# Linear attention and a mixture of experts: chunks attended in pairs, tokens transposed in idle banks

## Chip, cores, metric

One NeuronCore of a Trainium2 chip runs the whole kernel as one program. The metric is the device time of an execution in microseconds (us), least is best; the median of the runs shown is used.

## What is computed

Attention with decay over 4 batches of 768 tokens, 8 heads of 64, and on its output x (3072 tokens of 512) a mixture of 8 experts, of which each token uses the best:

```
for b in range(nb):
    intra = einsum('bhic,bhjc->bhij', qb, kb) * Dmask     # Dmask[i,j] = lam**(i-j) for i >= j
    intra = einsum('bhij,bhjd->bhid', intra, vb)
    inter = einsum('bhid,bhde->bhie', qb * lam_pow, kv_state)
    out[:, :, sl] = intra + inter
    kv_state = lam_block * kv_state + einsum('bhsd,bhse->bhde', kb * rev_pow, vb)
...
logits = x @ w_gate + modality_bias[modality_id]
e_idx = argmax(logits, axis=1)
for e in range(E):
    mask = e_idx == e
    h = maximum(x[mask] @ w1[e], 0.0)
    out[mask] = gate_w[mask, None] * (h @ w2[e])
...
```

gate_w is the softmax weight of the chosen expert; w1 is 512 x 1024 and w2 1024 x 512 for each expert.

## The kernel before

The engines: TensorE (PE; PEld loads its weights), VectorE (DVE), ScalarE (ACT), GpSimd (POOL), SyncE (SP, issues most DMAs). PSUM has eight banks of 128 x 512 float32 in which PE writes.

The attention takes 24 chunks of 128 tokens (six a batch), one in each step of a loop over g. A step has, on PE: the scores of chunk g (L224, 64 x 128 tiles, into two banks named s); what chunk g − 1 reads from the carried state (L267, bank o; not for the first chunk of a batch); its outputs (L280, into the same o); and the carry of chunk g (L241, keys times values, bank kv; not for the last chunk of a batch). DVE multiplies the scores by the decay mask (L229, two operations of 128 x 512, tiles pt), prepares the faded queries qd and keys kd of the next chunk (L196, L206) and adds the carried state (L252) to what POOL faded (L250). ACT copies the outputs to xt (L282).

For three chunks at a time tokens() transposes xt (L290, banks x and s), ACT copies the result to xn (L293), and it is stored to xs in memory. gate() multiplies the three chunks by the gate weights (L304, 96 columns). DVE transposes the logits (L312), and for each finished batch route() and route_places() find the expert and the place of every token with some twenty small operations of 0.1 to 0.4 us (L329 to L378); PE ranks the tokens in between (L357 to L362). The result sloti is a slot in the table inv for each token; write_slots (L383, POOL) writes it, one chunk a step (two a step for some steps). sloti is one tile: the next batch's may be computed only when all six writes of the batch before have landed. After the second batch early_list() counts (L393) and lists the first two wide tiles from tokens already routed.

The experts: a wide tile is 256 tokens of one expert. Its weights and tokens are split into a high and a low part (ACT casts, L545; DVE subtracts, L546), and every product is three matmuls (L660, L663, L664). wide() makes the hidden layer in four halves hp (bank s; hh by ACT L680, hl by DVE L684), second() multiplies by w2. Two tiles from the early list come first, then two thin ones and ten or more wide ones from the late list, which needs the last batch's routing: the ranking and the count (L393) stand between the first tile's matmuls, the list is made on DVE behind them, and the rest are fetched by it.

Banks: three s, two x, one kv, two o. What the program writes without an order of its own is ordered by a scheduler, which places an instruction where its inputs are expected; behind(later, first, wait=False) ties one instruction behind another in that order, without a wait. Each engine runs its own instructions strictly in order.

## Time and profile before

| what | us |
|---|---|
| median of 3 runs | 387.98 (386.94 to 388.87) |
| the profiled execution | 387.84 |
| its span in the trace | 386.2 |
| first wide tile's first matmul (L660) | 98.47 |
| ranking of the last batch (L357) | 111.09 |

PE is busy nearly throughout, at the full of its two clock levels (granted share 1.00 in every stretch of 10 us up to 110). In the rows, a start and a length in us come first, then engine, line, operation, the tile written and those read, the shape, and how many instructions the row stands for; in brackets how long the engine was idle before it, and what ended that. One matmul of the program shows as two records here, and records overlap: the time that a run takes is the difference of the starts of two rows.

### The profile page before, as it was taken

To read this page: it belongs to the slowest core of one execution; us is meant where nothing else is said; L and a number is where in the kernel's file an instruction comes from. 1 tells how busy PE (TensorE), PEld (TensorE's weight loads), DVE (VectorE), ACT (ScalarE), POOL (GpSimd) and SP (SyncE) were. 2 spreads that over 40 slices of the span, in tenths; PEclk is the share of its full clock that TensorE was granted. 3 is DMA by queue.
4 is the path that set the end of the run, shared out by engine and by line. 5 is a ranking of instruction groups with operands and counts; after the bars stand their busy time and mean duration, and the time that the engine had idled before them with its cause. 6 is when DMAs were issued, how large, how long until landed. Compare 5 with 4: busy or idle time off the path is not lost.

```text
span 386.2 us, 9952 instructions
## 1 busy us (share of the span) xinstructions
PE 378.7 (98%) x3722; PEld 336.5 (87%) x3722; DVE 267.1 (69%) x469; ACT 183.6 (48%) x277; POOL 188.6 (49%) x176
## 2 busy tenths in 40 slices
PE   8999999999999999999999999999999999999993
PEld 5888888888998977898989899898989899898982
DVE  7879867988898531667594857669494857759430
ACT  1323333235872523564564827366573736547430
POOL 2621332736607411475757484756658385663101
PEclk9999999999999999999999999999999999999998
DMA  7999999996800286110238796311212121101101
GB/s 278 409 387 411 407 410 396 330 391 209 300 2 22 80 280 235 24 45 27 50 104 247 210 281 209 107 35 63 41 63 37 68 36 55 42 27 62 52 2 52
DMA packets 34571, 62.59 MB, mean 162 GB/s; under 512 B 17611, under 2 KB 18125, under 8 KB 34512
## 3 DMA queue, kind: packets, MB, share of 16 engines
q1 hardware_dynamic: 28832, 49.15, 36.9%
q0 software_dynamic: 5680, 12.70, 10.0%
q8 instruction: 31, 0.51, 0.5%
q14 instruction: 28, 0.23, 0.2%
HBM read 90.49 MB, written 13.67 MB: 270 GB/s over the span
## 4 chain that ended last, share of the span: by engine, by line
PE 50%; issue 22%; POOL 12%; DMA 5%; POOLq 4%; DVE 3%; SPq 2%; ACT 1%; DVEq 0%; ACTq 0%
POOL xg L596 8%; PE o L280 6%; PE s L224 6%; PE s L664 4%; PE s L660 4%; PE s L663 4%; PE o L660 4%; PE o L664 4%; PE o L663 4%; POOLq L990 4%; POOL out_dram L756 4%; PE o L267 3%; PE kv L241 2%; PE x L290 2%; DMA inv<-pay,sloti 2%
## 5 line engine op out<-in xcount | busy, mean ns | idle before, releaser
L596 POOL DMA_INDIRECT xg<-xs,quarters x72 | 97.9, 1360 | 33.3 <-issue 20.1
L660 PE MATMUL s<-xh,w1h 128*128 128x256 f32 x384 | 107.5, 280 | 0.0
L664 PE MATMUL s<-xh,w1l 128*128 128x256 f32 x384 | 107.4, 280 | 0.0
L663 PE MATMUL s<-xl,w1h 128*128 128x256 f32 x384 | 107.1, 279 | 0.0
L660 PE MATMUL o<-w2h,hh 128*128 128x512 f32 x192 | 75.3, 392 | 0.0
L663 PE MATMUL o<-w2l,hh 128*128 128x512 f32 x192 | 74.9, 390 | 0.0
L664 PE MATMUL o<-w2h,hl 128*128 128x512 f32 x192 | 74.9, 390 | 0.0
L684 DVE SCALAR_TENSOR_TENSOR hl<-s,hh 128x512 fp32r<-128x512 f32 x48 | 33.2, 691 | 58.0 <-ACT hh L680 50.4
L660 PEld LDWEIGHTS s<-xh,w1h 128*128 128x128 f32 x384 | 72.3, 188 | 0.6 <-issue 0.2
L663 PEld LDWEIGHTS s<-xl,w1h 128*128 128x128 f32 x384 | 72.3, 188 | 0.4
L664 PEld LDWEIGHTS s<-xh,w1l 128*128 128x128 f32 x384 | 72.3, 188 | 0.1
L546 DVE TENSOR_TENSOR w2l<-raw,w2h 128x1024 fp32r<-128x1024 f32 x48 | 58.8, 1225 | 12.2 <-ACT w2h L545 12.2
L680 ACT ACTIVATE hh<-s 128x512 fp32r<-128x512 f32 x48 | 28.7, 598 | 67.0 <-PE s L664 67.0
L756 POOL DMA_INDIRECT out_dram<-y,idx x20 | 29.1, 1455 | 61.0 <-ACT y L755 32.6
L546 DVE TENSOR_TENSOR w1l<-raw,w1h 128x1024 fp32r<-128x1024 f32 x48 | 56.3, 1208 | 2.4 <-ACT w1h L545 2.3
L545 ACT CAST w2h<-raw 128x1024 fp32r<-128x1024 f32 x48 | 50.0, 1042 | 0.0
L545 ACT CAST w1h<-raw 128x1024 fp32r<-128x1024 f32 x48 | 48.3, 1051 | 0.8 <-ACT w2h L545 0.7
L664 PEld LDWEIGHTS o<-w2h,hl 128*128 128x128 f32 x192 | 36.1, 188 | 7.5
L660 PEld LDWEIGHTS o<-w2h,hh 128*128 128x128 f32 x192 | 36.1, 188 | 7.4 <-issue 0.4
L663 PEld LDWEIGHTS o<-w2l,hh 128*128 128x128 f32 x192 | 36.1, 188 | 7.0
L383 POOL DMA_INDIRECT inv<-pay,sloti x24 | 25.7, 1070 | 31.2 <-DVE sloti L368 11.4
L282 ACT COPY xt<-o 128x256 f32<-128x256 f32 x48 | 17.6, 372 | 46.8 <-PE o L280 45.7
(201 smaller groups left out, 449.3 us busy)
## 6 DMA issues: line engine op xcount, KB each, us to landing
raw<-in_w_dram SPq DMA_DIRECT2D x104, 512.0 KB
load<-in_qkv_dram SPq DMA_DIRECT2D x18, 1024.0 KB
load<-in_qkv_dram SPq DMA_DIRECT2D x12, 512.0 KB
xs<-xn SPq DMA_DIRECT2D x24, 256.0 KB
w1h<-in_w_dram SPq DMA_DIRECT2D x4, 512.0 KB
spare<-in_w_dram SPq DMA_DIRECT2D x4, 512.0 KB
xg<-xs,quarters POOLq DMA_INDIRECT x72, 3.3
quarters<-inv SPq DMA_DIRECT2D x36, 1.0 KB
```

Source lines behind the costliest of these rows:

```text
L224: mm = nc.tensor.matmul(sps[hl][:, p, :], kt[r, p, :], qt[r, p, :], start=True, stop=True)
L280: mm = nc.tensor.matmul(op[half][place(p, hl), i, :], vt[:, (2 * p + hl) * D : (2 * p + hl + 1) * D], pts[hl][:, p, :], start=(c == 0 and ...
L383: sc = nc.gpsimd.indirect_dma_start(out=inv, out_offset=bass.IndirectOffsetOnAxis(ap=at, axis=0), in_=pay[:, c, :], in_offset=None)
L545: cp = nc.scalar.copy(out=hi, in_=src)
L546: df = nc.vector.tensor_tensor(out=lo, in0=src, in1=hi.bitcast(F32), op=ALU.subtract)
L596: last = nc.gpsimd.indirect_dma_start(out=xg[:, g * P : (g + 1) * P], out_offset=None, in_=xs.rearrange("n (r k) -> (n r) k", r=4)[: 4 * r ...
L660: mm = nc.tensor.matmul(out, ah, bh, start=first, stop=False)
L663: nc.tensor.matmul(out, ah, bl, start=False, stop=False)
L664: return nc.tensor.matmul(out, al, bh, start=False, stop=last)
L680: act = nc.scalar.activation(out=hh[i], in_=hp, func=AF.Relu)
L684: low.append(nc.vector.scalar_tensor_tensor(out=hl[i], in0=hp, scalar=0.0, in1=hh[i].bitcast(F32), op0=ALU.max, op1=ALU.subtract))
L756: sc = nc.gpsimd.indirect_dma_start(out=out, out_offset=bass.IndirectOffsetOnAxis(ap=idx[:, t, 0:1], axis=0), in_=y, in_offset=None, bound ...
```

## The change

From chunk 6 on (FIRST = NC) a step takes a pair of chunks: scores of both, what both read from the state, the tokens of the pair before, its gate, the carry of the first, the outputs of both, the carry of the second. Groups for tokens and gates are pairs (GROUP = 2), so there are twelve gates of 64 columns instead of eight of 96. The masks of a chunk are one operation over a tile of two banks, of which there are two (BANKS), and one x bank is left. The tokens of a pair are transposed in the kv and the x bank. Small routing operations are tied behind a step's preparations (last). The last pair's tokens and gate stand in the first wide tile, behind its first half (last_tokens), and the tile's own tokens are turned ahead of the last pair's outputs. The halves of a hidden layer go to s, s and kv in turn (one_bank); two of hh share a tile.

```diff
@@ -27,14 +27,15 @@
 CAP = N
 EARLY = 2
 SOON = B - 2
+FIRST = NC
 MIN_WIDE = 10
 MAX_WIDE = 17
 LIST = len(THIN) + MAX_WIDE + 2
 PAD = 16384
 Q = P // 4
 SW = 8
-GROUP = 3
-BANKS = {"s": 3, "x": 2}
+GROUP = 2
+BANKS = {"s": 2, "x": 1}
 FEW = sum(THIN)
 EMPTY = E * CAP // TT
...
+        def two_banks(nm):
+            return ps.tile([P, 2, DM], F32, name=nm, bufs=BANKS[nm])
 
         def scores(g, after=None):
             kt, qt, vt, kn = loaded(g)
-            pts = []
-            sps = [ps.tile([P, NP, P], F32, name=nm, bufs=BANKS[nm]) for nm in (("s", "x") if g == 1 else ("s", "s"))]
+            sp = two_banks("s")
             for p in range(NP):
                 for hl, r in enumerate(halves2):
-                    mm = nc.tensor.matmul(sps[hl][:, p, :], kt[r, p, :], qt[r, p, :], start=True, stop=True)
+                    mm = nc.tensor.matmul(sp[:, hl, p * P : (p + 1) * P], kt[r, p, :], qt[r, p, :], start=True, stop=True)
                     if after is not None:
                         behind(mm, after, wait=False)
-            for hl in range(2):
-                pt = work.tile([P, NP, P], F32, name="pt", bufs=4)
-                op = nc.vector.tensor_tensor(out=pt, in0=sps[hl], in1=dk[:, hl], op=ALU.mult)
-                pts.append(pt)
-            return pts, op
-
...
+        def from_states(some, after=None):
+
+            op = [ps.tile([P, len(some), NP // 2, P], F32, name="o", bufs=2) for _ in range(2)]
+            begun = False
+            for n, g in enumerate(some):
+                c = g % NC
+                st, qd = state[c % 3], qds.get(g)
+                if c > 0:
+                    for i in range(NP // 2):
...
+            return op, begun, after
+
+        def outputs(some, op, begun, after=None):
+            g = some[0]
             if g % GROUP == 0:
                 gathered[g // GROUP] = work.tile([P, GROUP, NP, P], F32, name="xt", bufs=2)
-            xt = gathered[g // GROUP][:, g % GROUP]
+            xt = gathered[g // GROUP][:, g % GROUP : g % GROUP + len(some)]
+            for n, g in enumerate(some):
+                vt, pt = loaded(g)[2], st1.pop(g)
+                for half in range(2):
+                    for i in range(NP // 2):
+                        p = half * (NP // 2) + i
+                        for hl in range(2):
+                            mm = nc.tensor.matmul(op[half][place(p, hl), n, i, :], vt[:, (2 * p + hl) * D : (2 * p + hl + 1) * D],
+                                             pt[:, hl, p, :], start=(i == 0 and n == 0 and not begun),
+                                             stop=(i == NP // 2 - 1 and n == len(some) - 1))
+                            if after is not None:
+                                behind(mm, after, wait=False)
+                st2[g] = xt[:, n]
+                after = mm
             for half in range(2):
-                for i in range(NP // 2):
-                    p = half * (NP // 2) + i
-                    for hl in range(2):
-                        mm = nc.tensor.matmul(op[half][place(p, hl), i, :], vt[:, (2 * p + hl) * D : (2 * p + hl + 1) * D],
-                                         pts[hl][:, p, :], start=(c == 0 and i == 0), stop=(i == NP // 2 - 1))
-                copies.append(nc.scalar.copy(out=xt[:, half * (NP // 2) : (half + 1) * (NP // 2), :], in_=op[half]))
-            return xt, mm
...
+        def tokens(some, before=None, apart=False):
+
+            if apart:
+                xp = [bank("kv", 1), bank("x", BANKS["x"])]
+            else:
+                xp = two_banks("s")
+                xp = [xp[:, i] for i in range(2)]
+            for i, g in enumerate(some):
+                xt = st2.pop(g)
+                for p in range(NP):
+                    mm = nc.tensor.transpose(out=xp[i][:, p * P : (p + 1) * P], in_=xt[:, p, :], identity=ident)
+                    if before is not None:
+                        behind(mm, before, wait=False)
+            for i, g in enumerate(some):
+                xn = work.tile([P, DM], F32, name="xn", bufs=4)
+                copies.append(nc.scalar.copy(out=xn, in_=xp[i]))
+                stores.append(nc.sync.dma_start(out=xs[g * P : (g + 1) * P, :], in_=xn))
+            return mm
+
         def gate(n, after):
 
-            lp = ps.tile([P, GROUP, Q], F32, name="x", bufs=BANKS["x"])
...
 
 
-        def count_tiles(first, nm):
-
-            cp = ps.tile([P, E], F32, name="x", bufs=BANKS["x"])
-            nc.tensor.matmul(cp, onesb, ohsum, start=True, stop=True)
+        def count_tiles(first, nm, before=None, last=None):
+
+            cp = two_banks("s")[:, 0, :E]
+            mm = nc.tensor.matmul(cp, onesb, ohsum, start=True, stop=True)
+            if before is not None:
+                behind(mm, before, wait=False)
             cnt = const.tile([1, E], F32, name="cnt" + nm)
-            nc.vector.tensor_copy(out=cnt, in_=cp[0:1, :])
...
-        def turn_early(before=None, part=range(2), tag="x"):
-            for i in part:
-                tp = ps.tile([P, 2, TT], F32, name=tag, bufs=BANKS[tag])
+        def turn_early(before=None, part=range(2), tag="s"):
+            whole = two_banks("s") if tag == "s" else ps.tile([P, 1, DM], F32, name="x", bufs=BANKS["x"])
+            tps = [whole[:, n].rearrange("p (a t) -> p a t", a=2) for n in range(len(part))]
+            for i, tp in zip(part, tps):
                 for j in range(2):
                     for t in range(2):
                         mm = nc.tensor.transpose(out=tp[:, j, t * P : (t + 1) * P], in_=block(xt0[t], 2 * i + j),
                                                  identity=ident)
                         if before is not None:
                             behind(mm, before, wait=False)
-                split(tp, xh[i], xl[i])
+            for i, tp in zip(part, tps):
+                halved.append(split(tp, xh[i], xl[i]))
             return mm
 
...
-        high, low, second_high, second_low = [], [], [], []
+        high, low, second_high, second_low, halved, turn = [], [], [], [], [], [0]
+
+        def one_bank():
+
+            turn[0] += 1
+            return ps.tile([P, DM], F32, name="kv", bufs=1) if turn[0] % 3 == 0 else two_banks("s")[:, 0]
 
         def wide(tail, before=None, ordered=False, between=None):
 
             for i in range(4):
-                hp = ps.tile([P, 2, TT], F32, name="s", bufs=BANKS["s"])
+                hp = one_bank().rearrange("p (a t) -> p a t", a=2)
...
+            routes = None
             if g == 4:
-                passed = tokens(2, st2.pop(2), passed)
-            if g < ng:
-                st1[g], masked = scores(g, passed if g in (2, 4) else None)
...
+            if g < FIRST:
+                st1[g], masked, passed = scores(g, passed)
+            elif g < ng and g % 2 == 0:
+                for c in (g, g + 1):
+                    last = masked
+                    st1[c], masked, passed = scores(c, passed)
+                    behind(masked, last, wait=False)
...
             if g == ng - 1:
-                split(raw1[0], w1h[0], w1l[0], late=True)
-            elif g == ng:
-                split(raw1[1], w1h[1], w1l[1], late=True)
-                for c in sorted(st2):
-                    tokens(c, st2.pop(c))
-                turn_early(tag="s")
+                for made, urgent in zip(split(raw1[1], w1h[1], w1l[1], late=True), halved[-1]):
+                    behind(made, urgent, wait=False)
...
+            elif g < ng and g % 2 == 0:
+                op, begun, passed = from_states([g, g + 1], passed)
+                passed = tokens([g - 2, g - 1], passed, True)
+                parts_of, passed = gate(g // GROUP - 1, passed)
+                last = masked
+                if g + 2 < ng:
+                    kds[g + 2] = fade_keys(g + 2, masked)
+                    if (g + 2) % NC:
+                        qds[g + 2] = fade_queries(g + 2, prepared[-1])
+                    last = prepared[-1]
+                else:
+                    split(raw1[0], w1h[0], w1l[0], late=True)
+                    passed = turn_early(passed)
+            elif g < ng:
+                if g % NC < NC - 1:
+                    passed = carry(g, kds[g], passed, last)
+                    last = updates[-1]
+                if g + 2 < ng:
+                    prepare(g + 2, last)
+                    last = prepared[-1]
+                passed = outputs([g - 1, g], op, begun, passed)
+                routes = add_logits(*parts_of, last)
+                if g + 1 < ng:
+                    passed = carry(g + 1, kds[g + 1], passed, last)
...
-            if routed is not None:
-                slots = route_places(*routed)
-            routed = routes
+            if g == FIRST - 1:
+                make_bias(logits[-1])
+            if routed is not None and g < ng and g % 2:
+                slots = route_places(*routed, last=last)
+                routed = None
+            routed = routes or routed
 
             few = 2 if early < g < early + 4 or g >= ng else 1
             write_slots(slots[:few], passed)
             slots = slots[few:]
 
             if g == early + 2:
-                exA, nA = early_list()
...
+        def last_tokens(mm):
+
+            nonlocal routed
+            mm = tokens([ng - 2, ng - 1], mm)
+            parts_of, mm = gate(ng // GROUP - 1, mm)
+            routed = add_logits(*parts_of)
+            return mm
+
         def run(n):
             nonlocal before
             idx = idxs.get(n) or get_idx(n)
-            begun, _ = wide(tail, before, n >= wides, between if n == wides else None)
+            begun, _ = wide(tail, before, n >= wides, {0: last_tokens, wides: between}.get(n))
             before = None
             if n == 0:
                 write_slots(route_places(*routed, begun))
                 late_list(exA, nA)
                 turn_early(begun)
                 for i in range(4):
-                    split(raw1[i], w1h[i], w1l[i])
+                    for op, urgent in zip(split(raw1[i], w1h[i], w1l[i]), (high, low)):
+                        behind(op, urgent[min(i + 1, 3)], wait=False)
                 fetch_w2(*regs(n + 1))
                 at = fetch_few_rows()
                 idxs[wides] = get_idx(wides)
```

Lines move: scores L224 to L235, mask L229 to L239, from-state L267 to L280, outputs L280 to L298, carry L241 to L251, tokens L290 to L321, gate L304 to L338, sloti L368 to L402, slot writes L383 to L421, count L393 to L431, matmuls of the tiles L660/L663/L664 to L704/L707/L708, ohsum L378 to L416, casts L545 to L587, subtractions L546 to L588.

Order on PE, chunks 14 and 15, before (L224 scores, L267 from the state, L280 outputs of the chunk before, L241 carry):

```order
L224 MATMUL s<-load 128x128 x8
L267 MATMUL o<-qd,state_126 64x128 x8
L280 MATMUL o<-pt,load 64x128 x8
L241 MATMUL kv<-load,kd 64x64 x8
L224 MATMUL s<-load 128x128 x8
L267 MATMUL o<-qd,state_127 64x128 x8
L280 MATMUL o<-pt,load 64x128 x8
L241 MATMUL kv<-load,kd 64x64 x8
```

After, the pair 14 and 15 (L235, L280, tokens L321 and gate L338 of the pair before, L251, L298):

```order
L235 MATMUL s<-load 128x128 x16
L280 MATMUL o<-qd,state_127 64x128 x8
L280 MATMUL o<-qd,state_125 64x128 x8
L321 MATMUL kv<-ident,xt 128x128 x4
L321 MATMUL x<-ident,xt 128x128 x4
L338 MATMUL s<-xt,gates 32x64 x16
L251 MATMUL kv<-load,kd 64x64 x8
L298 MATMUL o<-pt,load 64x128 x16
L251 MATMUL kv<-load,kd 64x64 x8
```

Each kind now stands once for two chunks, and tokens and gate come in every pair.

Order on POOL where the first batch's last slot writes stand, before (L383 write, L250 fading of a state):

```order
L383 DMA inv<-pay,sloti 24832x8 [waits PE_49]
L250 TENSOR_TENSOR faded<-state_127,pq 128x256 [waits DVE_49]
L383 DMA inv<-pay,sloti 24832x8 [waits PE_49]
L250 TENSOR_TENSOR faded<-state_125,pq 128x256 [waits DVE_49]
L250 TENSOR_TENSOR faded<-state_126,pq 128x256 [waits DVE_49]
L383 DMA inv<-pay,sloti 24832x8 [waits DVE_49,PE_49]
```

After (L421, L260):

```order
L421 DMA inv<-pay,sloti 24832x8 [waits PE_49]
L260 TENSOR_TENSOR faded<-state_127,pq 128x256 [waits DVE_49]
L421 DMA inv<-pay,sloti 24832x8 [waits PE_49]
L260 TENSOR_TENSOR faded<-state_125,pq 128x256 [waits DVE_49]
L421 DMA inv<-pay,sloti 24832x8 [waits PE_49]
L260 TENSOR_TENSOR faded<-state_126,pq 128x256 [waits DVE_49]
L421 DMA inv<-pay,sloti 24832x8 [waits DVE_49,PE_49]
```

The last write of the first batch is the third row before and the fifth after, one fading later. The wait for PE of that write is for the carry of chunk 14 (L241) before, and for the gate in pair 14 and 15 (L338) after.

Order on DVE around the slots of the second batch, before (L368 sloti, L229 mask, L395 on: early list):

```order
L364 TENSOR_TENSOR pos<-oh,x 128x48 [waits PE_49]
L375 RECIPROCAL pay<-sm 128x6 [waits DVE_49]
L378 TENSOR_TENSOR ohsum<-ohsum,ohn 128x8
L366 TENSOR_REDUCE slot<-pos 128x6 [waits DVE_49]
L368 SCALAR_TENSOR_TENSOR sloti<-m_1086,slot 128x6 [waits DMASW3_49,DMASW2_49,DMASW4_49,DMASW1_49,DMASW5_49,DMASW0_49,DVE_49]
L229 TENSOR_TENSOR pt<-s,dk 128x512 [waits PE_49] x2
L196 TENSOR_TENSOR qd<-load,pq 128x512 [waits DMAHW0_49]
L252 TENSOR_TENSOR state_127<-faded,kv 128x256 [waits PE_49,Pool_49]
L395 COPY cntA<-x 1x8 [waits PE_49]
```

After (L402 sloti, L239 masks of 16 and 17):

```order
L398 TENSOR_TENSOR pos<-oh,x 128x48 [waits PE_49]
L416 TENSOR_TENSOR ohsum<-ohsum,ohn 128x8
L400 TENSOR_REDUCE slot<-pos 128x6 [waits DVE_49]
L402 SCALAR_TENSOR_TENSOR sloti<-m_1079,slot 128x6 [waits DMASW3_49,DMASW2_49,DMASW4_49,DMASW1_49,DMASW5_49,DMASW0_49,DVE_49]
L239 TENSOR_TENSOR pt<-s,dk 128x1024 [waits PE_49] x2
L207 TENSOR_TENSOR kd<-load,dk 128x512 [waits DMAHW4_49]
L196 TENSOR_TENSOR qd<-load,pq 128x512 [waits DMAHW5_49]
L207 TENSOR_TENSOR kd<-load,dk 128x512
L346 STREAM_TRANSPOSE lg<-s 128x64 [waits PE_49]
L435 COPY cntA<-s 1x8 [waits PE_49]
```

The slots stand ahead of the masks in both; after, the early list stands behind all preparations of its pair, and both masks are one row of two operations of 1024.

Order on DVE at the end of the first wide tile's hidden layer, before (L546 splits, L378 the sum of the chosen experts, L395 its count):

```order
L546 TENSOR_TENSOR w2l_1934<-raw_137,w2h_1932 128x1024 [waits DMAHW1_49,Activation_49]
L684 SCALAR_TENSOR_TENSOR hl_1944<-s,hh_1940 128x512 [waits Activation_49]
L364 TENSOR_TENSOR pos<-oh,x 128x48 [waits PE_49]
L378 TENSOR_TENSOR ohsum<-ohsum,ohn 128x8
L546 TENSOR_TENSOR w2l_1934<-raw_138,w2h_1932 128x1024 [waits DMAHW2_49,Activation_49]
L366 TENSOR_REDUCE slot<-pos 128x6 [waits DVE_49]
L395 COPY cntB<-x 1x8 [waits PE_49]
```

After (L588, L416, L435):

```order
L588 TENSOR_TENSOR w2l_1874<-raw_136,w2h_1872 128x1024 [waits DMAHW2_49,Activation_49]
L733 SCALAR_TENSOR_TENSOR hl_1882<-s,hh_1878 128x512 [waits Activation_49]
L398 TENSOR_TENSOR pos<-oh,x 128x48 [waits PE_49]
L588 TENSOR_TENSOR w2l_1874<-raw_137,w2h_1872 128x1024 [waits DMAHW3_49,Activation_49]
L400 TENSOR_REDUCE slot<-pos 128x6 [waits DVE_49]
L416 TENSOR_TENSOR ohsum<-ohsum,ohn 128x8
L588 TENSOR_TENSOR w1l_143<-raw_131,w1h_139 128x1024 [waits DMAHW5_49]
L402 SCALAR_TENSOR_TENSOR sloti<-m_1952,slot 128x6 [waits DMASW5_49,DMASW4_49,DMASW6_49,DMASW2_49,DMASW7_49,DMASW0_49,DVE_49]
L435 COPY cntB<-s 1x8 [waits PE_49]
```

The sum ohsum stood ahead of the last split of w2, and stands behind it.

## Rows read from the trace of the kernel before

**Rows 1.** Page, part 1: busy time, share of the span, instructions of PE.

```profile
PE 378.7 (98%) x3722; PEld 336.5 (87%) x3722; DVE 267.1 (69%) x469; ACT 183.6 (48%) x277; POOL 188.6 (49%) x176
```

**Rows 2.** PE timeline, chunks 10 to 12; xN below 16 is a run's rest.

```profile
41.01 1.09 PE L280 MATMUL o<-pt,load 128*64 128x128 f32 x16
41.93 0.64 PE L241 MATMUL kv<-load,kd 128*64 128x64 f32 x16
42.49 1.09 PE L290 MATMUL x<-ident,xt 128*128 128x128 f32 x8
43.42 0.60 PE L290 MATMUL s<-ident,xt 128*128 128x128 f32 x4
43.95 0.87 PE L304 MATMUL x<-xt,gates 128*32 128x96 f32 x32
44.75 1.16 PE L224 MATMUL s<-load 64*128 64x128 f32 x16
45.08 0.84 PE L224 MATMUL s<-load 64*128 64x128 f32 x12
45.30 0.61 PE L224 MATMUL s<-load 64*128 64x128 f32 x8
45.84 0.67 PE L267 MATMUL o<-qd,state 64*64 64x128 f32 x16
46.44 1.09 PE L280 MATMUL o<-pt,load 128*64 128x128 f32 x16
```

**Rows 3.** PE timeline, first and last of three long score runs.

```profile
67.73 1.75 PE L224 MATMUL s<-load 64*128 64x128 f32 x16
...
86.10 1.47 PE L224 MATMUL s<-load 64*128 64x128 f32 x16
```

**Rows 4.** Chain of waits (start, us, what), then DVE's timeline, around chunk 16.

```profile
59.02 7.77 DMA inv<-pay,sloti
...
66.91 0.17 DVE L368 SCALAR_TENSOR_TENSOR sloti<-m,slot 128x6 int32<-128x6 f32 x1 [1.99 <-DMA inv<-pay,sloti]
```

**Rows 5.** The tile inv, all 24 slot writes: time from issue to landing.

```profile
DMA to landing us min/median/max: 2.1/5.4/6.1
```

**Rows 6.** DVE timeline, masks, early list, and two slow operations.

```profile
67.00 1.28 DVE L229 TENSOR_TENSOR pt<-s,dk 128x512 f32<-128x512 f32 x2
68.19 0.68 DVE L196 TENSOR_TENSOR qd<-load,pq 128x512 f32<-128x512 f32 x1
69.12 0.15 DVE L395 COPY cntA<-x 1x8 f32<-1x8 f32 x1
...
73.84 1.27 DVE L229 TENSOR_TENSOR pt<-s,dk 128x512 f32<-128x512 f32 x2
...
81.88 0.87 DVE L196 TENSOR_TENSOR qd<-load,pq 128x512 f32<-128x512 f32 x1
82.67 1.10 DVE L206 TENSOR_TENSOR kd<-load,dk 128x512 f32<-128x512 f32 x1
```

**Rows 7.** Timelines of DVE, ACT and PE in the first wide tile.

```profile
97.49 1.29 DVE L546 TENSOR_TENSOR xl<-s,xh 128x512 fp32r<-128x512 f32 x2 [0.24 <-ACT xh L545]
...
113.55 0.16 DVE L378 TENSOR_TENSOR ohsum<-ohsum,ohn 128x8 bf16<-128x8 bf16 x1
113.72 1.23 DVE L546 TENSOR_TENSOR w2l<-raw,w2h 128x1024 fp32r<-128x1024 f32 x1
...
112.65 1.04 ACT L545 CAST w2h<-raw 128x1024 fp32r<-128x1024 f32 x1
...
111.28 0.49 PE L660 MATMUL o<-w2h,hh 128*128 128x512 f32 x1
...
113.89 0.18 PE L393 MATMUL x<-ohsum,onesb 128*128 128x8 bf16 x1
```

**Rows 8.** Timelines of POOL and PE: last few tokens gathered, and turned.

```profile
129.99 1.01 POOL L954 DMA_INDIRECT xq<-xs,idxq  x1 [3.88 <-DMA idx<-inv]
...
134.62 0.63 PE L771 MATMUL x<-ident,xq 96*128 96x96 f32 x4
```

## What I predict

> **What bounds the kernel now.** I read the page's first part, then TensorE's timeline, then the chain of waits and the timelines of the engines that feed TensorE. PE is busy for 98% of the span [rows 1] and no wait of it in the attention is worth a term, so only three things can move the end: fewer or cheaper PE instructions, the gaps between them, and stalls. The whole change lies ahead of the middle of the first wide tile; from there on all five engines keep their order, so a microsecond there is a microsecond at the end.
>
> The gaps are in [rows 2]. Chunk 11's sixteen score records take 1.09 us from their start to the next kind's (44.75 to 45.84). But the row cut at twelve begins at 45.08, the one cut at eight at 45.30: two pairs in 0.22, 0.11 a pair, so eight pairs are 0.90 and 0.20 us is lost wherever a run of scores begins or ends. Single starts in the other runs, read the same way, lose 0.16 for a run from the state (L267), 0.145 for outputs with their carry (L280, L241), 0.147 for a run of transposes (eight and four take 0.93 + 0.53), 0.14 for a gate (0.80 for 32 records). Each kind uses the array in another shape (the figure pairs in the rows), and the loss is one for each run, however long.
>
> **Fewer runs.** Up to the ranking of the last batch, before has 23 score runs, 20 from-state, 24 output-and-carry, 11 transpose and 8 gate runs; after has 14, 14, 15, 14 and 12. So −9 × 0.196 − 6 × 0.162 − 9 × 0.145 + 3 × 0.147 + 4 × 0.142 = −3.03 us. Scores, outputs, carries and transposes keep their counts.
>
> **Gates.** 12 of 64 columns instead of 8 of 96. Nothing shows a gate of 64. By columns (the 64-column carries at 41.93 step at 0.06 a pair [rows 2], and the 96-column gate at its own rate) a gate without its loss is 0.46 against 0.66: 12 × 0.46 − 8 × 0.66 = +0.2. If it cannot start records faster than the 96-column one, it stays 0.66: +2.6. I take +0.2, since four kinds of run go by their columns, and keep 2.6 for the range.
>
> **Old stalls.** Three score runs in before are longer than 1.09: 67.73 by 0.59, 71.04 by 0.43, 86.10 by 0.31 ([rows 3] has the first and the last). They wait for a score bank that DVE frees, and DVE is late by small routing operations ahead of a mask; at 66.91 it had itself waited 1.99 us for a slot write [rows 4]. A pair's masks have some 5 us until PE's outputs need them, so these go: −1.33. The question is what is late next.
>
> **The slot write comes back.** In before the sixth write of batch 0 starts 0.27 us behind a carry, and its landing 7.77 us later releases DVE's next slot computation [rows 4]. The six writes go out one a chunk; in after the sixth waits for the gate in pair (14, 15), and the next batch's slots (L402) still stand ahead of pair (16, 17)'s masks on DVE. With D from the write's start to its landing, DVE does after that gate: 0.27 + D + 0.2, masks of 16 and 17 (2.4: four widths of 512 at 0.6, 67.00 to 68.19 [rows 6]), three prepared keys and queries of the same width 1.8, logits 0.2, the early list 2.7 (69.12 to 73.84 less two masks, one kd and one transpose), mask 18 at 1.2: D + 8.8. The gate of pair (18, 19) writes the two-bank tile that mask 18 frees. PE gets there after 2.83 (kv, outputs, kv), ranking 0.22, scores 1.99, from-state 1.03, transposes 1.02, gate 0.60, count 0.15, outputs and carry 2.36, scores 1.99, from-state 0.60, transposes 1.02: 13.8 us. So the stall is D − 5.0. These writes landed in 5.4 to 6.1 us, at least 2.1 [rows 5], and once in 7.77: 0.4 to 1.1, and 2.8. I take D = 6.2, between the usual and that one: +1.2. The next gate is held by mask 20, which comes no later than PE does then; nothing is added there.
>
> The Trainium skill, page "DMA: Bandwidth & Descriptors", section "Anatomy of one DMA — SWDGE (gpsimd) path", gives a fixed cost of about 2.0 us and little more for so few bytes. By it this stall would be nothing and the sum 1.2 us less. The shortest landing here, 2.1 us, agrees with it; the 7.77, under a full load queue, does not.
>
> **First wide tile.** Its turned tokens now lie in one two-bank tile, so ACT's second xh waits for DVE's first xl, where before the two xl ran back to back in 1.29 us (97.49) [rows 7], and both stand behind the first w1 cast and w1l. Counted from the scores of 22: last token copy done at 4.85, w1h cast 5.9, w1l 7.0, xl 7.6, xh 8.2, xl 8.9; PE wants it at 8.4 to 8.55: +0.5.
>
> The late list's count is the larger piece. In before ohsum (113.55) stands ahead of the last w2l (113.72, 1.23 us), and the count at 113.89 waits for nothing [rows 7]. In after it stands behind that w2l. PE makes the third half of hp ahead of the second, but ACT still takes the second first. So from X, the end of the second, ACT has three hh (0.5, half the width of a cast), three w2h and two w1h casts (1.04 at most, 0.95 back to back): X + 6.5; w2l and two small operations: X + 8.05. PE has 24 matmuls at 0.118, the ranking, and 16 of the second at 0.23 (eleven take 2.6): X + 6.65. +1.4, and behind it on PE stand the transposes of tile 1 and the rest of the second.
>
> The list made from that count ends with a gather, started at 129.99 and used at 134.62 without a wait [rows 8]; by my reading of the order the list takes 0.85 longer from the count while PE reaches the use 0.8 sooner. I count nothing, and up to 0.5 if its landing takes more than 3 us.
>
> Put at nothing: loads (after the first chunk PE waits for none, and pairs ask some 2 us sooner) and tokens in the kv bank, whose copy ends, by my reading, just before the next carry wants the bank; both would show on PE at once.
>
> **Sum.** The profiled execution took 387.84 (span 386.2), 0.14 under the median. 387.84 − 3.03 + 0.2 − 1.33 + 1.2 + 0.5 + 1.4 = **386.8 us**, 1.2 under the median of 387.98. A measurement of this kernel can tell about 0.5% from no change, 1.94 us: below 386.04 is faster, above 389.92 slower. So the forecast is no change that can be told, on the fast side.
>
> **Rivals.** (a) The writes land quickly and the tile's stalls are as worked out: 386.8 − 1.2 = 385.6. For it: the 2.1 us of [rows 5], and the write comes a little later in a load queue that is emptying. Against: 7.77 at just this place. This is also what the skill's rule makes of it.
> (b) Nothing new stalls, the scheduler's order being absorbed by slack that I undercount: 386.8 − 1.2 − 0.5 − 1.4 = 383.7. Against it: each stall rests on an order that is fixed.
> (c) The gates do not get cheaper, so that the change does not give what fewer runs promise: 386.8 + 2.4 = 389.2, still no change by the bound.
> (d) Slower: DVE becomes the bound of a pair's step. A pair needs two masks 2.4, four keys and queries 2.4 and some 2.2 of states, transposes and half a batch's routing: 7.0 us, PE 7.0 to 7.7. While GpSimd worked, a query took 0.87 and a key 1.10 us instead of 0.68 [rows 6]. At 0.9 to 1.0 the four take 1.2 more, DVE 8.2 against PE 7.0 to 7.7: 0.5 to 1.2 in each of the five pairs (12 to 21) beside which GpSimd writes slots or fetches lists, about +4: 390.8. It decides from about 0.75 us a piece on. Against: of 39 keys and queries on DVE in before three were longer than 0.75 us, these two among them.
>
> **How the numbers follow.** Forecast 0.43 (alone 385.8 to 388.5: D from 5.4 to 7.8), (a) 0.20, (b) 0.12, (c) 0.11, (d) 0.14. Faster: (a), (b) and 0.05 of the forecast's own lower edge, 0.37. Slower: (d) and a little of (c), 0.15. Same: 0.48. The range leaves out half of (b) and half of (d) and some of (c)'s upper end: 384.0 to 389.8.
>
> **What the profile after would show.** Score rows of 32 records at about 2.0 us; a gate row start to start at 0.60 (right) or 0.80 (c). DVE's L402 near 68 us with a wait for the slot write, and PE's gate of pair (18, 19) or the scores before it late by about 1 us; no wait there is (a). In the first tile, an idle PE ahead of L707 and of the count L431 that waits for DVE's ohsum. Keys and queries of 0.9 us and masks late in most pairs would be (d). The prediction is wrong if PE is late where I put nothing: the kv bank's carry, the loads, the turned tokens' gather.

## The result, and the profile after

| | us |
|---|---|
| before, median of 22 runs | 387.35 (386.94 to 389.34) |
| after, median of 22 runs | 389.91 (388.25 to 393.61) |
| ratio, 95% interval | 1.0063 (1.0045 to 1.0081) |
| after, the profiled execution (its span) | 391.58 (390.0) |
| ranking of the last batch on PE, before and after | 111.09, 114.12 |

The kernel became slower by 0.6%, 2.6 us, where 386.8 was forecast. The profiled run of after is 1.7 us above its median; times after differ more from run to run than those before.

The page's first part, PE's row, after (busy, share of the span, instructions):

```profile
PE 378.4 (97%) x3850; PEld 337.3 (86%) x3850; DVE 269.2 (69%) x449; ACT 180.0 (46%) x259; POOL 192.5 (49%) x176
```

Against [rows 1] PE has 128 matmul records more (four gates more of 16 matmuls, two records each) and as many weight loads more, 256 instructions in all, and as much busy time. So the time went mainly into waiting, and the waits of PE from 10 to 112 us say where (the first four; the view leaves out those under 0.15 us):

```profile
engine line waited for: us in total, times, longest us
PE s L338 <- issue: 1.9, 1, 1.9
PE s L338 <- DVE pt L239: 0.6, 1, 0.6
PE o L298 <- issue: 0.5, 1, 0.5
PE s L235 <- issue: 0.3, 1, 0.3
```

The same view of before lists none. The word issue means that PE waited for nothing that the profile shows: no semaphore, no engine, no bank. The largest of these stands inside a gate, between two of its 32 records that need the same things. PE's timeline there:

```profile
70.66 0.60 PE L321 MATMUL x<-ident,xt 128*128 128x128 f32 x4
71.19 0.64 PE L338 MATMUL s<-xt,gates 128*32 128x64 f32 x28
73.75 0.42 PE L338 MATMUL s<-xt,gates 128*32 128x64 f32 x4 [1.91 <-issue]
74.10 0.19 PE L431 MATMUL s<-ohsum,onesb 128*128 128x8 bf16 x1
74.22 3.40 PE L298 MATMUL o<-pt,load 128*64 128x128 f32 x32
77.46 0.63 PE L251 MATMUL kv<-load,kd 128*64 128x64 f32 x16
```

PE stops at 71.83 with four records of the gate left, goes on at 73.75, and then the outputs of 74.22 take 3.24 us to the next row, where the same 32 records take 1.75 elsewhere. Windows of half a microsecond tell why (PE, PEld, DVE, ACT, POOL busy, then granted clock, DMA share, GB/s):

```profile
71.50:72.00 0.50, 0.33 (x22) 0.17 (x11) 0.50 (x2) 0.50 (x2) 0.33 (x1) 1.00 0.97 377
72.00:72.50 0.50, 0.00 (x0) 0.00 (x0) 0.50 (x2) 0.29 (x1) 0.50 (x1) 1.00 1.00 393
...
73.50:74.00 0.50, 0.25 (x4) 0.18 (x4) 0.14 (x1) 0.00 (x0) 0.00 (x0) 0.79 0.92 340
74.00:74.50 0.50, 0.50 (x9) 0.39 (x7) 0.28 (x2) 0.00 (x0) 0.05 (x1) 0.50 0.97 368
...
76.50:77.00 0.50, 0.50 (x8) 0.50 (x6) 0.47 (x8) 0.00 (x0) 0.17 (x1) 0.50 0.07 22
77.00:77.50 0.50, 0.50 (x12) 0.50 (x10) 0.39 (x5) 0.35 (x1) 0.00 (x0) 0.80 1.19 131
```

After the idle stretch the granted clock is at its lower level, 0.50 (1.2 GHz), from 73.8 to 77.2. So this one stop cost 2.1 us itself and 1.5 us behind it.

**What the stops have in common.** A queue of instructions among the DMA queues carries PE's program to it. The page counts 32 packets and 0.52 MB on it, 16 KB a packet. The DMA view of 71.2 to 72.4 us has this row (queue, kind: packets, MB, share):

```profile
q8 instruction: 1, 0.02, 5.1%
```

and from 72.4 to 73.7 there is none. Each stop of after ends 1.3 to 1.5 us behind the end of such a packet (this one 1.43). And it ends at the same place of the program, counted in PE's instructions. Windows from the start to each of the four stops behind 20 us:

```profile
0.00:23.84 23.84, 21.97 (x347) 16.62 (x347) 19.05 (x37) 6.30 (x13) 10.78 (x33) 1.00 0.92 351
0.00:29.83 29.83, 27.66 (x474) 21.57 (x475) 21.72 (x42) 8.75 (x19) 11.40 (x34) 1.00 0.94 357
0.00:66.04 66.04, 62.82 (x1237) 53.18 (x1237) 54.06 (x111) 18.91 (x40) 23.56 (x47) 1.00 0.99 383
0.00:73.74 73.74, 68.60 (x1364) 58.26 (x1364) 59.66 (x124) 21.10 (x44) 25.53 (x49) 1.00 0.99 377
```

PE and PEld together: 694, 949, 2474, 2728. The view leaves out semaphore instructions and the like (11, 14, 23, 25 by then); with them it is 705, 963, 2497 and 2753, which is 449 plus 1, 2, 8 and 9 times 256 (the second two off). So a packet carries 256 instructions (64 bytes each, by its 16 KB), and **PE stops because it has none left until the next packet arrives**. Where PE has done all it holds, I call it a pause; pauses are added up from 9 us to the ranking. After has 3.7 us of them (0.29, 0.57, 0.74 and 2.13, from the start of the last record to that of the next), before 0.23, in one.

The packets start late while the key loads fill the DMA engines through which they go. A row each of before and after, 40 to 60 us, shows what both have in common and what not:

```profile
40.00:60.00 20.00, 20.00 (x394) 17.52 (x394) 15.23 (x36) 7.42 (x17) 8.00 (x9) 1.00 1.03 407
```

```profile
40.00:60.00 20.00, 20.00 (x437) 18.29 (x437) 17.23 (x37) 6.85 (x14) 7.86 (x8) 1.00 1.03 406
```

DMA is full in both (1.03). PE issues 394 matmul records in before and 437 in after: fewer idle stretches between runs, and more gates. The earliest that a packet of before starts up to the ranking is at 158 of these 449 instructions. That leaves 290, which last 7.4 us at the rate of before and 6.6 at that of after. Up to 87 us a packet waits 2.9 to 4.7 us in before (from the instruction 158 to its start), takes about 1.0, and 1.43 later PE goes on: 7.1 at the worst. That is an estimate from these rows; it leaves before 0.3 us and after −0.5.

The rate is not all of it. In after the packets wait longer, too: 3.3 to 5.4 us, and 7.0 for the one of 71.34, behind which the longest pause stands. Had that one waited 4.7 us, the longest of before, the pause of 2.13 would by the same estimate be gone, and with it, it seems, the lower clock. Why it waited 7.0 is not shown.

### The profile page after: what moved, and what is told of

It reads as the page before. It is cut to its first block, busy times and chain, and to the rows that moved or that the text cites. A ratio compares the mean times of both kernels' runs of the same rounds, so it can differ in the third digit from the quotient of the medians.

```text
span 390.0 us, 10172 instructions
## 1 busy us (share of the span) xinstructions
PE 378.4 (97%) x3850; PEld 337.3 (86%) x3850; DVE 269.2 (69%) x449; ACT 180.0 (46%) x259; POOL 192.5 (49%) x176
## 4 chain that ended last, share of the span: by engine, by line
PE 71%; issue 11%; DMA 10%; POOL 5%; DVE 1%; ACT 1%; SPq 0%; POOLq 0%; ACTq 0%
PE o L704 8%; PE o L707 8%; PE o L708 8%; PE s L708 6%; PE s L704 6%; PE s L707 6%; PE o L298 5%; PE s L235 4%; DMA load<-in_qkv_dram 4%; DMA mod<-in_modality_dram 3%; PE kv L704 3%; PE kv L707 3%; PE kv L708 3%; POOL inv L421 3%; PE o L280 2%
## 5 line engine op out<-in xcount | busy, mean ns | idle before, releaser
L638 POOL DMA_INDIRECT xg<-xs,quarters x72 | 100.5, 1396 | 30.8 <-issue 20.4
L704 PE MATMUL o<-w2h,hh 128*128 128x512 f32 x192 | 75.1, 391 | 0.0
L707 PE MATMUL o<-w2l,hh 128*128 128x512 f32 x192 | 74.9, 390 | 0.0
L708 PE MATMUL o<-w2h,hl 128*128 128x512 f32 x192 | 74.7, 389 | 0.0
L704 PE MATMUL s<-xh,w1h 128*128 128x256 f32 x264 | 73.9, 280 | 0.0
L707 PE MATMUL s<-xl,w1h 128*128 128x256 f32 x264 | 73.7, 279 | 0.1
L708 PE MATMUL s<-xh,w1l 128*128 128x256 f32 x264 | 73.6, 279 | 0.0
L588 DVE TENSOR_TENSOR w2l<-raw,w2h 128x1024 fp32r<-128x1024 f32 x48 | 58.8, 1225 | 12.5 <-ACT w2h L587 12.5
L588 DVE TENSOR_TENSOR w1l<-raw,w1h 128x1024 fp32r<-128x1024 f32 x48 | 56.5, 1214 | 3.7 <-ACT w1h L587 3.7
L707 PEld LDWEIGHTS s<-xl,w1h 128*128 128x128 f32 x264 | 49.6, 188 | 0.6 <-DVE xl L588 0.3
L587 ACT CAST w2h<-raw 128x1024 fp32r<-128x1024 f32 x48 | 50.0, 1043 | 0.0
L704 PEld LDWEIGHTS s<-xh,w1h 128*128 128x128 f32 x264 | 49.6, 188 | 0.5 <-issue 0.2
L708 PEld LDWEIGHTS s<-xh,w1l 128*128 128x128 f32 x264 | 49.6, 188 | 0.0
L733 DVE SCALAR_TENSOR_TENSOR hl<-s,hh 128x512 fp32r<-128x512 f32 x33 | 22.8, 691 | 37.5 <-ACT hh L729 37.5
L587 ACT CAST w1h<-raw 128x1024 fp32r<-128x1024 f32 x48 | 48.2, 1051 | 0.0
L421 POOL DMA_INDIRECT inv<-pay,sloti x24 | 26.9, 1121 | 33.0 <-DVE cntB L435 9.2
L704 PEld LDWEIGHTS o<-w2h,hh 128*128 128x128 f32 x192 | 36.1, 188 | 7.5 <-issue 0.4
L708 PEld LDWEIGHTS o<-w2h,hl 128*128 128x128 f32 x192 | 36.1, 188 | 7.6
L707 PEld LDWEIGHTS o<-w2l,hh 128*128 128x128 f32 x192 | 36.1, 188 | 7.0
L729 ACT ACTIVATE hh<-s 128x512 fp32r<-128x512 f32 x33 | 19.7, 598 | 45.6 <-PE s L708 43.5
L704 PE MATMUL kv<-xh,w1h 128*128 128x256 f32 x120 | 33.7, 281 | 0.0
```

The lines of the kernel that those rows point to most:

```text
L421: sc = nc.gpsimd.indirect_dma_start(out=inv, out_offset=bass.IndirectOffsetOnAxis(ap=at, axis=0), in_=pay[:, c, :], in_offset=None)
L587: cp = nc.scalar.copy(out=hi, in_=src)
L588: df = nc.vector.tensor_tensor(out=lo, in0=src, in1=hi.bitcast(F32), op=ALU.subtract)
L638: last = nc.gpsimd.indirect_dma_start(out=xg[:, g * P : (g + 1) * P], out_offset=None, in_=xs.rearrange("n (r k) -> (n r) k", r=4)[: 4 * r ...
L704: mm = nc.tensor.matmul(out, ah, bh, start=first, stop=False)
L707: nc.tensor.matmul(out, ah, bl, start=False, stop=False)
```

## Experiments

The theories in the expectations: S, the slot write makes the loss; F, PE runs out of instructions behind a packet; then, of the cause of late packets, B (loads in bursts) and D (the rate at which PE uses instructions). Each run of a kernel was timed beside the kernel before on the same chip, and ratios are to that.

**Was it the slot write?** A second buffer for the slots of a batch, so that DVE needn't wait for the landing:

```diff
-            sloti = t2("sloti", I32)
+            sloti = work.tile([P, NC], I32, name="sloti", bufs=2)
```

> The changed kernel with two buffers for the slot tile sloti instead of one, so that DVE's slots of a batch no longer wait until the slot writes of the batch before have landed. In the trace of the changed kernel DVE waits 1.56 us there (until 69.41), and PE then stands still from 71.83 to 73.75 with nothing that the profile shows as its cause. Theory S (the step of the prediction: the landing of the slot writes makes the masks late and with them PE): the wait on DVE goes, PE's pause behind chunk 17's gate goes with it, 1 to 3.5 us less than the changed kernel's 389.9, so 386.4 to 388.9. Theory F (PE has run out of instructions: in all four pauses without a shown cause it resumes 1.43 us after a 16 KB packet of the instruction queue has ended): DVE's wait goes too, PE's pauses stay, each 1.4 us behind an instruction packet, and the time is 389.5 to 390.3.

Measured: 390.20 us, ratio 1.0067 (1.0042 to 1.0093), as after itself. S falls. The profiled run, at 388.69 below that median, had pauses at 23.95, 30.21, 43.32 and 90.24, 3.0 us in sum, each behind a packet, though no slot write held DVE any more. The two longest in the waits of PE from 10 to 112 us:

```profile
PE kv L251 <- issue: 1.1, 1, 1.1
PE s L235 <- issue: 0.6, 1, 0.6
```

**Does the pause hang on the place in the program?** Six of the ten matmuls at the start (L865) are left out and 64 of eight columns added, 58 matmuls more ahead of everything, which moves all that follows by 116 instructions:

```diff
+            for i in range(64):
+                nc.tensor.matmul(nothing[:, :8], busy[:, :P], busy[:, :8], start=(i == 0), stop=(i == 63))
...
-        keep_busy(10)
+        keep_busy(4)
```

> The changed kernel with four long matmuls and 64 short ones (8 columns) in place of the ten long ones with which PE idles at the start, so that all later PE instructions stand 116 places later in the instruction stream, with nothing else changed. Theory F: the blocks of instructions end at other places of the attention, each some 2.8 us of work earlier; the pauses near 29, 65 and 72 us are found elsewhere or are gone, new ones may stand where there were none, each resuming about 1.4 us behind an instruction packet; time 387 to 391. Theory S: the pause behind chunk 17's gate stays where it is, time as the changed kernel within 0.7 us.

Measured: 391.67, ratio 1.0119 (1.0089 to 1.0149), a little over what F allowed. PE's timeline shows that the gate no longer pauses, and outputs 13 us earlier do:

```profile
57.71 0.83 PE L298 MATMUL o<-pt,load 128*64 128x128 f32 x11
60.30 0.87 PE L298 MATMUL o<-pt,load 128*64 128x128 f32 x12 [1.76 <-issue]
```

All six pauses of this run end at 449 plus a multiple of 256. So the pause belongs to the block of instructions, not to the gate, its bank or its inputs: F holds.

**Loads.** Chunk loads issued two steps later, so that fewer would be under way:

```diff
-            if 1 <= g <= ng - LOADS:
-                load_chunk(g + LOADS - 1)
+            if 3 <= g <= ng - LOADS + 2:
+                load_chunk(g + LOADS - 3)
```

> The changed kernel with chunk loads issued two steps later (four chunks ahead of the attention instead of six), so that the load queue is not full all the time up to 80 us. Theory F (PE's instructions come through DMA engines that the chunk loads keep full): instruction packets start earlier relative to PE's need, the pauses of PE near 29, 65 and 72 us shrink from 0.35, 0.5 and 1.9 us by more than half in sum, and the following stretch at half clock (74 to 77 us) goes: 386 to 388.5. Theory S: the slot write lands sooner as well, DVE's wait of 1.56 us shrinks and PE's pause with it: 387 to 389. If PE instead waits for chunk loads, scores start late by whole microseconds with that releaser, and the time is over 391.

Measured: 393.28, ratio 1.0132 (1.0103 to 1.0160), a miss: DMA stayed full, and pauses grew to 6.7 us, eight of them.

Loads in halves, each held until the third one ahead of it has landed (in after, and in before as a control), and until the second one:

```diff
-            load_part(g, slice(0, 2))
+            for part in (turned, plain):
+                load_part(g, part)
+                behind(loads[-1], loads[-1 - 3])
```

> The changed kernel with the loads from chunk 6 on in halves of 512 KB, each of which waits until the half three before it has landed, so that at most 1.5 MB of loads stand in the DMA engines' queues. Where chunks are loaded in the changed kernel, an instruction packet starts when PE has issued 320 to 420 records beyond the last block's place (160 where no loads run), and PE stands still whenever it comes to 449 before the packet has ended by 1.43 us. Theory F (instructions wait behind chunk loads): packets start at 320 or fewer, the pauses of 0.3 to 2.1 us at 24, 30, 66 and 74 us go, 386 to 388. If packets wait for something else than the queued loads: same starts, same pauses, 389.5 to 391.5.

> The kernel before the change with the same limit of three halves. Its PE comes close to the end of its instructions (packets start at 280 to 370) but stands still only once, 0.23 us at 23.4. Theory F: little is to be had, 386.8 to 387.8; and the pause of 0.59 us near 67.7 to 68.3, which the mask ends behind a slot write, shrinks if that write lands sooner. If the limit itself costs time (SyncE waits, stores behind it), it shows here by itself: over 388.

> As the one with three halves, but each half waits for the half two before it: at most 1 MB of loads in the queues. Theory F: instruction packets start earlier still, at 280 or fewer, and no pause of PE ends 1.4 us behind one; but the loads now run at the pace of their latency, and may come late for the scores of the last chunks: 385.5 to 388, over 389 only if scores wait for loads, which the trace would name.

Measured: 398.48 (1.0282, 1.0249 to 1.0315), 398.95 (1.0292, 1.0251 to 1.0332) and 413.86 (1.0680, 1.0662 to 1.0698). Pauses went (0.28, 0 and 0): with less under way, packets of after started up to 80 us on average at 286 instead of 346 of their 449 instructions. But new waits of PE for DVE and ScalarE of 2 to 6 us came, so the limit costs more than it gives; what these two waited for was not followed further. With the limit of three, after is level with before (398.48 and 398.95), where without it after is 0.6% slower; as both are held up elsewhere, this fits F and does not prove it.

Untransposed keys not loaded from chunk 6 on, values used in their place (both kernels compute something else there, and are compared with each other only):

```diff
-            load_part(g, slice(0, 2))
+            load_part(g, turned)
+            loads.append(nc.sync.dma_start(out=chunks[g][:, plain, :1], in_=source(g)[:, plain, :1]))
...
-            return kt, qt, t[:, 1, 0], t[:, 1, 1]
+            return kt, qt, t[:, 1, 0], t[:, 1, 1 if g < LOADS else 0]
```

> The changed kernel with a quarter of each chunk's load left out from chunk 6 on: the untransposed keys are not loaded, and the values are used in their place for the carry (so the carried states, tokens and routing are others, and the number of tiles may differ; to be compared with the kernel before, cut in the same way). Loads then ask some 220 GB/s instead of 290, beside 73 of stores, of about 410 that the queues moved when full. Theory F (PE's instructions wait in DMA engines filled by loads): packets start at 160 to 300 records beyond the last block's place instead of 320 to 420, no pause of PE ends 1.4 us behind one after 35 us, and the ranking of the last batch comes 3 to 5 us sooner than the changed kernel's 114.1. Any other cause that the loads do not touch (slots, masks, banks): the pauses stay, less than 1 us sooner.

> The kernel before the change, cut in the same way. It has nearly no pause of that kind, so theory F says that it gains little: the ranking of the last batch 0.5 to 1.5 us sooner than its 111.1 (the late masks near 68 and 71 us shrink with a sooner slot write), and stands 1.5 to 3 us behind the changed kernel cut in the same way, which is what fewer runs are worth once instructions come in time. If instead the changed kernel stays slower than this one, the gain that the prediction took from fewer runs (3.03 us) is not there.

Measured: 431.63 (428.45 to 434.06) and 430.07 (429.73 to 431.02): after is not below before here either, and a difference of 0.4% is within the spread of six and five runs. F is missed here: in after the pauses did not go (4.7 us, 0.25 in before), and its ranking, which was to come ahead of before's, came at 113.1 and before's at 110.4. The DMA engines were not relieved: up to 70 us their share was 0.89 to 1.01 in after. That the loads only ran further ahead is the likely reason, and is not shown.

**Is it the single mask?** Two operations of 512 in its place:

```diff
-            op = nc.vector.tensor_tensor(out=pt, in0=sp.rearrange("j h (p t) -> j h p t", p=NP), in1=dk, op=ALU.mult)
+            for hl in range(2):
+                op = nc.vector.tensor_tensor(out=pt[:, hl], in0=sp[:, hl].rearrange("j (p t) -> j p t", p=NP), in1=dk[:, hl],
+                                             op=ALU.mult)
```

> The changed kernel with each chunk's mask as two operations of 512 columns instead of one of 1024, as before the change. Where PE waits for a whole mask in the changed kernel (outputs of chunk 0, 0.30 us; gate ahead of the first pair's carry, 0.57 us), outputs may begin at half a mask, but the two-bank tile still comes free only with the second half: 0.2 to 0.4 us less at chunk 0, nothing at the gate, and some 0.1 us a pair more on DVE: 389.3 to 390.2. If the single mask were the main cause of the lost time, it would be 388 or less.

Measured: 391.65, ratio 1.0101 (1.0073 to 1.0129): no gain, over the 389.3 to 390.2 expected, and pauses of 5.5 us.

**Pairs from a later chunk on** (FIRST = 18, and 12), with single steps ahead, two-bank scores and gates of pairs:

> The changed kernel with chunks taken singly up to the eighteenth, as before the change (scores, from the state, outputs, carry), with tokens and the gates of 64 columns in each second step, and in pairs from there on, when few loads are left. Theory F: PE's pauses behind instruction packets become fewer and shorter than in the changed kernel but do not vanish, since the narrow gates add 64 records in each second step; part of the gain of fewer runs (last three pairs, about 0.35 us each) and the old late masks' end stays: 386.5 to 389. If pairs are not what makes the time worse, it is the changed kernel's 390 or more.

> The same with pairs from the twelfth chunk on, three pairs of them under full loads. Theory F: between the changed kernel and the one with pairs from the eighteenth, 387.5 to 390.

Measured: 399.54 (1.0304, 1.0281 to 1.0327) and 395.81 (1.0204, 1.0182 to 1.0227). Inconclusive: single steps with two score tiles of two banks wait for DVE (in the first kernel 3.6 us for the mask, L239, at one place and 2.4 for the transpose of the logits, L346, in four), a cost that neither before nor after has. Pauses were 0 and 2.5 us.

**Bursts or rate?** In after two loads are issued in a row, in before one a step. Spacing them in after, and pairing them in before:

```diff
+                if g >= FIRST and g % 2 == 0:
+                    behind(loads[-1], scored)
```

```diff
-            if 1 <= g <= ng - LOADS:
+            if g <= NC and 1 <= g <= ng - LOADS:
+                load_chunk(g + LOADS - 1)
+            elif g % 2 == 0 and g <= ng - LOADS:
+                load_chunk(g + LOADS - 2)
```

> The changed kernel, with the key loads of even steps held until the scores of that step's pair are computed, so that loads are issued one by one and not two at a time; nothing else is changed. Theory B (two loads in one burst stand ahead of TensorE's own instruction packets and make them start late): the packets start 20 to 100 records earlier than in the changed kernel, the pauses 1.4 us behind a packet shrink to under 1 us in sum, and the time is 387 to 389. Theory D (TensorE uses up its instructions faster with fewer idle stretches, whatever the loads do): packets start 320 to 419 records before the end of supply as in the changed kernel, pauses stay at 3 us or more, and the time is 389.5 to 391.5. If the held loads land late instead, TensorE waits for them at its gates, and the time is above 392.

> The kernel before, with the key loads behind the resident chunks issued two at a time on even steps; nothing else is changed. Theory B (bursts make instruction packets late): pauses 1.4 us behind a packet appear in the pass over chunks, 1 to 4 us in sum, packets start later than 370 records, and the time is 388 to 390. Theory D (only TensorE's own rate of use decides): packets start at 280 to 369 records as before, no such pauses beyond the one of 0.23 us, and the time is 387 to 388. Loads that come late at a gate would show as waits for a load at chunk starts and would be counted apart.

Measured: after_spread 389.74, ratio 1.0067 (1.0037 to 1.0096): no faster than after. Its pauses of 2.3 us lie between what B (under 1) and D (3 or more) expected. before_burst 392.48, 1.0137 (1.0111 to 1.0164), without a pause; its time goes into one wait at 23.35 us, since the first load of the new scheme comes late, and the lower clock behind it (0.50 for 3.4 us). The waits of PE in before_burst:

```profile
PE s L224 <- DMA load<-in_qkv_dram: 3.8, 1, 3.8
```

So bursts alone made no pauses in this run, and loads issued singly did not take them away in the other: B falls as the cause of all pauses. Whether bursts lengthen the longest waits of packets stays open: those were 5.2 us in after_spread and 7.0 in after, but 4.3 in before_burst.

**The rate alone.** In before each gate matmul of 96 columns is written as two (32 and 64), or as three of 32. Sums, order and loads are the same:

```diff
-                    mm = nc.tensor.matmul(lp[r], gates[:, k, :], x[:, :, k, r], start=(k == 0), stop=(k == NP - 1))
-                    behind(mm, after, wait=False)
+                    for cs in (slice(0, 1), slice(1, 3)):
+                        mm = nc.tensor.matmul(lp[r, cs], gates[:, k, :], x[:, cs, k, r],
+                                              start=(k == 0 and cs.start == 0), stop=(k == NP - 1 and cs.stop == GROUP))
+                        behind(mm, after, wait=False)
```

> The kernel before with each gate matmul of 96 columns written as two, of 32 and 64; the same sums, order, loads and idle stretches, and 32 records more in each of the eight gates, 256 in all, which is what the changed kernel's gates add. A gate takes at most 0.8 us where it took 0.66 if the 32 columns start as slowly as they can (16 at 0.01 more), so at most 1.2 us in all are its own. Theory D (TensorE uses up its instructions faster than packets of 256 records come): pauses 1.3 to 1.5 us behind a packet's end, at 449 records plus multiples of 256, appear in the pass over chunks, 0.5 to 3 us in sum, and the time is 388 to 390.5. Theory B (only bursts of loads make packets late): no such pauses, 387 to 388.5.

> The same with three matmuls of 32 columns, 512 records more in all. By columns a gate costs nothing more; if a matmul cannot start faster than one of 64 columns does (16 in 0.46 us), a gate takes 1.39 and all eight 5.8 us more, which stands in the gate's own rows and is taken off. Theory D: the pauses behind packets are as many as in the other kernel or more, at least 1 us in sum, unless the gates' slower starts lower the rate of use again. Theory B: none.

Measured: 393.91, ratio 1.0154 (1.0127 to 1.0182), and 403.22, 1.0411 (1.0365 to 1.0456). Both are more than expected of D, in the way it says. But the expectation counts wrongly: the change adds 128 matmul records and 128 weight loads (256 instructions, 32 packets for 31), and the first of these kernels 256 and 256 (512 instructions, 33 packets). The two largest waits of PE in the first, 15 to 100 us, and its timeline at the longest pause:

```profile
PE s L224 <- issue: 2.4, 3, 1.5
PE x L364 <- issue: 0.9, 1, 0.9
```

```profile
58.46 1.00 PE L305 MATMUL x<-xt,gates 128*32 128x32 f32 x64
59.40 0.71 PE L224 MATMUL s<-load 64*128 64x128 f32 x6
61.57 0.82 PE L224 MATMUL s<-load 64*128 64x128 f32 x10 [1.47 <-issue]
```

The ranking came at 117.32, 6.2 us later than before. A gate took 0.93 for 0.80, 1.0 us in eight; pauses, all at 449 plus a multiple of 256, came to 5.1. These two make up the difference. Up to 90 us packets waited 4.1 us on average and 5.7 at most, for 4.0 and 4.7 in before (4.7 and 7.0 in after), so here it is mainly the use that is faster. In the second a gate took 1.65 (6.8 in eight) and pauses 5.7, and the ranking came 12.6 later. So a kernel whose order, loads and banks are those of before pauses as after does, by 512 instructions more, twice what the change adds: D holds in kind. What 256 would cost in before was not run.

**The other way: fewer gate instructions in after.** One gate of 192 columns for each of the first three batches, and 128 and 64 columns for the last: 5 gates and 80 matmuls for 12 and 192 (after_mid: 7 gates, 112 matmuls). xt is one tile for six chunks:

```diff
-                gathered[g // GROUP] = work.tile([P, GROUP, NP, P], F32, name="xt", bufs=2)
+                gathered[g // NC] = work.tile([P, NC, NP, P], F32, name="xt", bufs=1)
...
-                parts_of, passed = gate(g // GROUP - 1, passed)
+                parts_of = None
+                if g % NC == 0:
+                    parts_of, passed = gate(g - NC, NC, passed)
+                elif g == ng - 2:
+                    parts_of, passed = gate(g - NC + 2, NC - 2, passed)
```

> The changed kernel with one gate of 192 columns for each of the first three batches, at the first pair of the next one, and two for the last batch (128 and 64 columns): 5 gates and 160 records for 12 gates and 384; the columns in sum are the same. By their columns the gates take 1.0 us less for seven fewer starts (7 x 0.14). Theory D (instructions run out): TensorE's pauses behind packets before 100 us, about 5 us with the lower clock in the profile of the changed kernel, shrink to under 2 us; ranking of the last batch at 108 to 111.5; time 384.5 to 387.5, under the kernel before. If the supply is not what the changed kernel's loss hangs on: 1.0 us less than the changed kernel, 388.5 to 389.5, with the pauses as they were. A wait of the next batch's copies to xt for the gate (one xt tile for six chunks) would show on ScalarE and then at TensorE's outputs, at 39, 67 and 95 us.

> The same, with two gates (128 and 64 columns) in every batch behind the first: 7 gates and 224 records. By columns 0.7 us less than the changed kernel. Theory D: between the changed kernel and the one with 160 records, pauses of 0 to 3 us, time 385 to 388. Without D: 388.7 to 389.7.

Measured: 402.12 and 404.00, where the kernel before took 406.67 on the same chip: ratios 0.9882 (0.9849 to 0.9915) and 0.9927 (0.9904 to 0.9950). Pauses were 0 and 1.1 us, as D expected. The ranking was not: it came at 117.1 and 117.3, where D had 108 to 111.5 for the first. After was not timed there, and no trace was taken of before at 406.67, so what these ratios owe to the gates is not shown. Both kernels have waits of their own; the largest in the first is 2.2 us at 33 us for a mask, behind a DVE that waited 3.0 us for the router's bias. It also has 1.9 us of idle time put down to issue between 75 and 99 us that stands behind no packet and is not explained. In the last run the bias is made later, and in steps without a gate the tokens are turned ahead of the states' matmuls:

```diff
+                gated = g % NC == 0 or g == ng - 2
+                if not gated:
+                    passed = tokens([g - 2, g - 1], passed, True)
                 op, begun, passed = from_states([g, g + 1], passed)
-                passed = tokens([g - 2, g - 1], passed, True)
+                if gated:
+                    passed = tokens([g - 2, g - 1], passed, True)
...
+                if g == FIRST + 1:
+                    make_bias(last)
```

> The version with 5 gates again, with two of its own waits taken out: the bias of the router is made on DVE two steps later (there DVE stood 3 us for its load, and TensorE 2.2 us behind it at 33 us), and in steps without a gate the tokens are turned ahead of what is read from the states, so that the copy out of the kv bank is hidden (0.5 us at 43, 65, 91 us). Theory D: pauses behind packets under 1.5 us in sum before 100 us, no wait of over 1 us before the ranking; 2 to 4 us under the version before it, 0.5 to 1.5% under that, and 1 to 2.5% under the kernel before on the same chip. If the supply is not the cause, it gains only those two waits and the gates' 1.0 us on the changed kernel: within 0.5% of the kernel before.

Measured, on a chip where before takes 387.48: 387.80 (386.73 to 389.05), ratio 1.0005 (0.9989 to 1.0022). That is some 0.6% under after and level with before. By the time alone it is what was expected if the supply were not the cause (within 0.5% of before); D had 1 to 2.5% under before. What speaks for D are the pauses: one of 0.9 us is left of 3.7, and the ranking came at 111.6, 2.5 us sooner than in after. In place of the others came waits for DVE (waits of PE from 10 to 125 us, the first three):

```profile
PE s L431 <- DVE pt L239: 2.0, 1, 2.0
PE s L338 <- DVE pt L239: 0.7, 1, 0.7
PE s L338 <- issue: 0.6, 1, 0.6
```

The first of them, in the chain of waits and on the timelines of DVE and PE:

```profile
63.07 7.33 DMA inv<-pay,sloti
...
70.53 0.17 DVE L402 SCALAR_TENSOR_TENSOR sloti<-m,slot 128x6 int32<-128x6 f32 x1 [3.14 <-DMA inv<-pay,sloti]
70.61 2.35 DVE L239 TENSOR_TENSOR pt<-s,dk 128x1024 f32<-128x1024 f32 x2
...
71.88 0.17 PE L431 MATMUL s<-ohsum,onesb 128*128 128x8 bf16 x1 [1.98 <-DVE pt L239]
```

That is the slot write of [rows 4], 7.33 us to its landing, and PE waits for the masks behind it. With after_few's gates and the two buffers of slots2 this wait should go; that kernel was not run, and that it would beat before is an estimate (the 2.0 us, from this run) and no result.

## Why the prediction was wrong

Up to the ranking the forecast's steps give −3.03 + 0.2 − 1.33 + 1.2 + 0.5 = −2.5; the ranking came 3.0 later. The miss there is 5.5 us. This is read in the profiled run; behind the ranking it lost 0.7 where 1.4 was forecast. The median, 389.91, is 3.1 over the forecast, 1.7 less than the profiled run, so in most runs the parts below must be smaller.

**The step that failed** is "only three things can move the end: fewer or cheaper PE instructions, the gaps between them, and stalls". It treats a closed gap as a gain, and the loads were put at nothing because PE waits for none. PE's own instructions come through the DMA engines that the loads fill, and their lateness is a fourth thing. The change closed gaps and added 256 instructions, so PE used what it held faster, and its packets waited longer as well. Pauses are 3.7 us in after for 0.2 in before, and the lower clock behind the longest costs 1.5: 5.0 of the 5.5. Of these, 3.6 hang on the one packet that waited 7.0 us, for a reason that stays open. That loads fill the DMA engines stood in the trace of before (a share of 1.03 from 10 to 70 us), and so did its one pause of 0.23 us; I passed over both.

**Fewer runs.** Right in kind: 32 score records take 1.98 us in after (67.15 to the next row at 69.13, below) where two runs of 16 take 2.18. In sum, runs and gates gave 2.2 us against the 2.8 counted, measured as what is left of the ranking's difference when pauses and waits are taken out on both sides.

```profile
67.15 2.06 PE L235 MATMUL s<-load 64*128 64x128 f32 x32
69.13 1.10 PE L280 MATMUL o<-qd,state 64*64 64x128 f32 x32
```

**Gates.** Right: 0.58 from start to start, where 0.60 was forecast for gates that go by their columns; rival (c) falls.

```profile
104.93 0.65 PE L338 MATMUL x<-xt,gates 128*32 128x64 f32 x32
105.51 0.39 PE L704 MATMUL kv<-xh,w1h 128*128 128x256 f32 x1
```

**Old stalls.** Right, all three of [rows 3] are gone. I had put nothing on a new one, a gate that waits for a whole mask of 1024:

```profile
33.20 0.65 PE L338 MATMUL s<-xt,gates 128*32 128x64 f32 x32 [0.57 <-DVE pt L239]
```

**The slot write, +1.2.** Wrong in after: DVE waited for it as forecast, and PE did not notice.

```profile
69.41 0.17 DVE L402 SCALAR_TENSOR_TENSOR sloti<-m,slot 128x6 int32<-128x6 f32 x1 [1.56 <-DMA inv<-pay,sloti]
69.49 2.35 DVE L239 TENSOR_TENSOR pt<-s,dk 128x1024 f32<-128x1024 f32 x2
```

The write of 63.74 landed at 69.3, 5.5 us later, and the masks were done just as PE came to the count at 71.8, had it not paused. In pair (18, 19), where I had put the stall, PE was 3.6 us late by its pause and the lower clock. That after_few2, which hardly pauses, waits 2.0 us behind this write (it landed 7.33 us later there) says that the hazard is real and its place was wrong: the count of pair (16, 17), which takes a score bank, not the gate of the next pair. By the Trainium skill ("DMA: Bandwidth & Descriptors", section "Anatomy of one DMA — SWDGE (gpsimd) path", about 2.0 us fixed) neither wait would be there; 5.5 and 7.33 us under full loads decide against it here.

**First wide tile.** xl behind xh: +0.5 forecast, and PE idles 0.2 ahead of L707 and loses 0.4 in all, right.

```profile
101.51 0.28 PE L704 MATMUL s<-xh,w1h 128*128 128x256 f32 x1
101.87 0.39 PE L707 MATMUL s<-xl,w1h 128*128 128x256 f32 x1
```

The count, +1.4, is wrong by all of it:

```profile
117.70 0.16 DVE L416 TENSOR_TENSOR ohsum<-ohsum,ohn 128x8 bf16<-128x8 bf16 x1
...
118.05 0.18 PE L431 MATMUL s<-ohsum,onesb 128*128 128x8 bf16 x1
```

The sum is done 0.2 us before PE wants it. That is no gift of PE's lateness: in after_few2, whose ranking comes 2.5 us sooner, the sum starts at 115.18 and the count at 115.53, without a wait. The step that failed is "PE makes the third half of hp ahead of the second". It makes half of it ahead: twelve matmuls into kv, the second half's 24 into s, and then the other twelve into kv.

```profile
106.91 0.28 PE L708 MATMUL kv<-xh,w1l 128*128 128x256 f32 x1
107.03 0.36 PE L704 MATMUL s<-xh,w1h 128*128 128x256 f32 x1
...
109.91 0.28 PE L704 MATMUL kv<-xh,w1h 128*128 128x256 f32 x1
```

So from X, the second's end (109.9), PE has 36 matmuls and not 24 ahead of the ranking, 1.4 us more at 0.118, and comes to the count at X + 8.1. DVE's sum is done at X + 8.0, as worked out (8.05).

**Gather of the last few tokens**, 0 to 0.5: PE waits for it, and the row stands 0.45 behind the one ahead of it; right.

```profile
137.51 0.28 PE L708 MATMUL s<-xh,w1l 128*128 128x256 f32 x1
137.96 0.72 PE L820 MATMUL x<-ident,xq 96*128 96x96 f32 x4 [0.17 <-DMA xq<-xs,idxq]
```

**Rival (d)** named a time near what came, 390.8, by a mechanism that did not: on DVE's timeline of after from 62 to 83 us no key or query is longer than 0.69 us.

Open: why packets wait longer in after than in before, and one of them 7.0 us; why a long pause is followed by the lower clock in one run and not in another (in after 1.9 us idle were; in shift 1.8 us were not), and how much of the spread of after's times from run to run this makes. Nor is the 0.6 us settled by which runs and gates gave less than counted.

## What to carry to other kernels

When a kernel's DMA engines are full, count PE's instructions as well as its columns: closing gaps or splitting matmuls can run it out of instructions, and the trace shows that as idle time that ends at "issue", a fixed time behind an instruction packet, at instruction numbers a fixed block apart. Wider matmuls in place of more of them cost nothing here (a gate of 192 columns took 1.44 us from start to start in after_few2, three of 64 take 1.74) and spare the supply. A stall counted at nothing, or at something, holds only as long as the rest of the schedule arrives when you think: the slot write cost PE nothing in after, and 2.0 us in a version in which most pauses were gone.

## What the hardware showed unexpectedly

PE's program comes in packets of 16 KB and 256 instructions through the DMA engines, beside the data, while the kernel runs: 31 of them in before, 32 in after, each some 1.0 us long while the chunks are attended. At the earliest a packet starts when some 290 instructions are left to PE, under full loads 30 (71.34 in after) to 170; a pause then ends 1.2 to 1.6 us behind the packet's end. 512 instructions more in before, in gates that cost 1.0 us more themselves, made it 6.2 us slower. And an idle PE of 1.9 us was followed in after by 3.4 us at the granted clock of 0.50, which cost 1.5 us more.
